# Two-layer recurrent-memory transformer: query, key and output products as 64-column pairs where the plan allows it, and seven groups of rows prepared early instead of five

## The chip, the core and the metric

The kernel runs on one core of a Trainium2 chip. The metric is the device time of one execution in microseconds (us); the time before is the median of four runs, 1634.55 us (1633.62 to 1636.03). Everything is planned when the program is built: the device executes a fixed list of instructions for each engine, without loops or branches.

## What is computed

Four blocks in a row: attention with a recurrent memory, a two-matrix feed-forward, then both again with the same weights. Cut to what matters:

```python
def A(x, mem, Wq, Wk, Wv, Wo):             # x: 2048 rows of 512, mem: 8 rows
    for s in range(64):                    # 64 segments of 32 rows, one after the other
        h = concat(mem, x[32*s:32*s+32])   # 40 rows
        q, k, v = h@Wq, h@Wk, h@Wv         # 32 heads of 128 columns
        p = softmax(masked(q @ k.T * scale))
        o = (p @ v) @ Wo                   # 40 rows of 512
        mem, out[s] = o[:8], o[8:]
def B(x): return relu(x@w1) @ w2           # 512 -> 1376 -> 512
x = x + A(norm(x)); x = x + B(norm(x))     # layer one
x = x + A(norm(x)); x = x + B(norm(x))     # layer two
```

The memory makes a chain: segment s+1 can't start before the first 8 output rows of segment s are there.

## The kernel before

**Tiling and order.** The two layers run interleaved, four segments apart (`DELTA` = 4). A step k handles segment k of layer one and segment k-4 of layer two, so there are 68 steps: 0 to 3 and 64 to 67 hold one layer, 4 to 63 hold both. In a two-layer step the two segments stand side by side as 80 columns of a tile `HT`, and one weight load serves both. The kernel keeps all four weight matrices in SBUF (4 MB each) and lives from TensorE (PE).

A step consists of: `step_values` (V = HT.T x Wv for the rows that are not prepared ahead; 64 weight columns, 512 moving columns, L973), `queries_keys` (Q and K per half unit of heads, 16 matmuls of 128 weight columns and 80 moving columns each, L1074; 16 such operations a step), `scores` (L1103, then the softmax on VectorE and ScalarE, and a transposition on PE at L646), `attend` (L1187) and `project` (32 heads x 4 column blocks into one PSUM bank, L1214). The copy at L1230 then moves the 8 memory rows of each layer to the next step's `HT`. Every second step a `finish_pair` runs the feed-forward for 64 rows of each layer (L646 and L766).

**Modes of PE.** A matmul addresses either the whole array (128 weight columns) or a part of its columns (64, or 32 in `values_narrow` at L992). Each operation is marked `WHOLE`, `COL64`, `COL32`, or `EITHER`; the last is emitted by the helper `across` (L642) as one 128-column matmul or as two 64-column ones, after the mode that PE is in. Values and scores are `COL64`; queries, keys and projections are `WHOLE`.

**The planner.** `Plan.order` (L320) simulates six resources with a cost for each operation, takes at each point the ready operation with the best priority (`PLACE`, `AHEAD`, `RULE` are numbers found beforehand), and charges `TURN` = 0.096 us for a change of PE's mode. Its result is the order in which each engine executes.

**Values prepared ahead.** Half the rows of a segment (its first 16) don't depend on the memory, so their V is computed for a group of four segments at once and stored in DRAM (`vh`), to be loaded into `V0` by a DMA in front of each step (`place_values`, L1003). Groups 0 to 5 (`EARLY` = 5) are prepared at the start, in the time in which the weights arrive, with 64-column matmuls (`early_values`, L926); the results of groups 1 to 5 wait in the room of `w1` and `w2`, which are loaded later. Groups 6 to 15 are prepared in five pairs during steps 4 to 53 (`late_values`, L937: 8 operations of 4 matmuls of 128 weight columns x 512, L944). Both kinds are `spare`: the planner may put them off. In steps 1 to 3, `values_narrow` makes the remaining V rows with 32 weight columns, evicts them into `vw`, and DMAs on SP's queue move them into `V0`.

**Start.** Weights are loaded in the order v, q/k, q/k, o, o through POOL's queue (`load_weights`, L488). Stores of the early groups follow on the same queue (L932), stores of their normalized rows `xh` on SP's queue after step 1's first loads (`put_op`), and `w1`/`w2` after that (`load_dense`, L503).

Of the kernel before, what the change touches and what calls it, by code (L numbers as in the profile page):

```python
# [26 lines left out]
WHOLE, COL64, EITHER, COL32 = range(4)  # L27
TURN = 0.096

RULE = (0.0731, 331.4491, 505.4188, 866559925356557.625)  # L30
PERIOD = 46.2777
PLACE = {
    ("attend.mmu0.0", 0): -152.667, ("attend.mmu0.0", 1): -118.912, ("attend.mmu0.0", 2): -639.225,
    ("attend.mmu0.0", 3): 328.193, ("attend.mmu0.0", 4): -173.499, ("attend.mmu0.0", 5): 386.967,
    ("attend.mmu0.0", 6): 449.133, ("attend.mmu1.0", 0): -183.38, ("attend.mmu1.0", 1): 433.744,
    ("attend.mmu1.0", 2): 361.711, ("attend.mmu1.0", 3): 441.403, ("attend.mmu1.0", 4): -122.568,
    ("attend.mmu1.0", 5): 199.077, ("attend.mmu1.0", 6): 581.404, ("attend.mmu2.0", 0): -862.741,
    ("attend.mmu2.0", 1): -762.821, ("attend.mmu2.0", 2): -99.412, ("attend.mmu2.0", 3): -218.396,
    ("attend.mmu2.0", 4): -720.778, ("attend.mmu2.0", 5): -60.014, ("attend.mmu2.0", 6): -142.579,
    ("attend.mmu3.0", 0): -166.299, ("attend.mmu3.0", 1): -129.893, ("attend.mmu3.0", 2): -1226.967,  # L40
    ("attend.mmu3.0", 3): 67.821, ("attend.mmu3.0", 4): -136.693, ("attend.mmu3.0", 5): -20.817,
    ("attend.mmu3.0", 6): 293.466, ("attend.mmu4.0", 0): 65.898, ("attend.mmu4.0", 1): -215.881,
    ("attend.mmu4.0", 2): 381.601, ("attend.mmu4.0", 3): 412.604, ("attend.mmu4.0", 4): -130.21,
    ("attend.mmu4.0", 5): -853.627, ("attend.mmu4.0", 6): 948.075, ("dense_layer.mm.0", 1): 732.94,
    ("dense_layer.mm.0", 3): 740.199, ("dense_layer.mm.0", 6): 839.326, ("dense_layer.mm.1", 1): -969.556,
    ("dense_layer.mm.1", 3): -286.677, ("dense_layer.mm.1", 6): 67.604, ("dense_layer.mm.2", 1): 398.19,
    ("dense_layer.mm.2", 3): 243.499, ("dense_layer.mm.2", 6): 419.477, ("dense_layer.mm.3", 1): 627.889,
    ("dense_layer.mm.3", 3): 181.496, ("dense_layer.mm.3", 6): 643.035, ("dense_layer.mm.4", 1): 161.37,
    ("dense_layer.mm.4", 3): 390.622, ("dense_layer.mm.4", 6): 400.054, ("dense_layer.mm.5", 1): 594.567,
    ("dense_layer.mm.5", 3): 753.248, ("dense_layer.mm.5", 6): 345.325, ("finish_pair.turn.0", 1): -144.39,  # L50
    ("finish_pair.turn.0", 3): -761.751, ("finish_pair.turn.0", 6): -878.802, ("g0", 2): -907.97,
    ("g1", 2): 259.128, ("g2", 2): -170.342, ("g3", 2): -266.685, ("g4", 2): -99.976, ("g5", 2): 565.774,
    ("late_values.mmv0.0", 0): 283.731, ("late_values.mmv1.0", 0): -248.92, ("late_values.mmv2.0", 0): -1018.714,
    ("late_values.mmv3.0", 0): 469.169, ("late_values.mmv4.0", 0): -1001.105, ("late_values.mmv5.0", 0): 1.489,
    ("late_values.mmv6.0", 0): -868.467, ("late_values.mmv7.0", 0): 433.155, ("layernorm.turn.0", 1): 337.759,
    ("layernorm.turn.0", 3): 441.922, ("layernorm.turn.0", 6): -292.588, ("layernorm.turn.1", 1): -863.663,
    ("layernorm.turn.1", 3): -167.818, ("layernorm.turnr.0", 0): -153.966, ("layernorm.turnr.0", 4): 426.349,
    ("layernorm.turnr.1", 0): 374.651, ("layernorm.turnr.1", 4): 594.017, ("prepare.turns.0", 2): -916.093,
    ("project.mm.0", 0): 352.884, ("project.mm.0", 1): 403.52, ("project.mm.0", 2): 426.265,
    ("project.mm.0", 3): 475.549, ("project.mm.0", 4): -8.363, ("project.mm.0", 5): 481.308,  # L60
    ("project.mm.0", 6): 364.213, ("project.mm.1", 0): 360.97, ("project.mm.1", 1): 250.905,
    ("project.mm.1", 2): 395.025, ("project.mm.1", 3): 90.611, ("project.mm.1", 4): -154.497,
    ("project.mm.1", 5): 342.487, ("project.mm.1", 6): -140.762, ("project.mm.2", 0): 69.475,
    ("project.mm.2", 1): 427.61, ("project.mm.2", 2): -910.526, ("project.mm.2", 3): 539.171,
    ("project.mm.2", 4): -962.774, ("project.mm.2", 5): 327.765, ("project.mm.2", 6): 570.292,
    ("project.mm.3", 0): 234.432, ("project.mm.3", 1): 212.581, ("project.mm.3", 2): 219.168,
    ("project.mm.3", 3): 1057.658, ("project.mm.3", 4): 374.948, ("project.mm.3", 5): 458.206,
    ("project.mm.3", 6): 1049.752, ("project.mm.4", 0): -906.842, ("project.mm.4", 1): -226.675,
    ("project.mm.4", 2): -119.077, ("project.mm.4", 3): 366.414, ("project.mm.4", 4): -955.316,
    ("project.mm.4", 5): 408.222, ("project.mm.4", 6): -222.974, ("queries_keys.mmu0.0", 0): -319.479,  # L70
    ("queries_keys.mmu0.0", 1): -311.142, ("queries_keys.mmu0.0", 2): -195.441,
    ("queries_keys.mmu0.0", 3): -783.942, ("queries_keys.mmu0.0", 4): -856.389,
    ("queries_keys.mmu0.0", 5): -1226.512, ("queries_keys.mmu0.0", 6): -189.749,
    ("queries_keys.mmu0.1", 0): -126.555, ("queries_keys.mmu0.1", 1): -875.245,
    ("queries_keys.mmu0.1", 2): -230.758, ("queries_keys.mmu0.1", 3): -218.806, ("queries_keys.mmu0.1", 4): -924.83,
    ("queries_keys.mmu0.1", 5): -998.214, ("queries_keys.mmu0.1", 6): -798.535, ("queries_keys.mmu0.2", 0): 1.933,
    ("queries_keys.mmu0.2", 1): -915.221, ("queries_keys.mmu0.2", 2): -763.206,
    ("queries_keys.mmu0.2", 3): -815.004, ("queries_keys.mmu0.2", 4): -155.478,
    ("queries_keys.mmu0.2", 5): -920.249, ("queries_keys.mmu0.2", 6): -766.935, ("queries_keys.mmu0.3", 0): -285.59,
    ("queries_keys.mmu0.3", 1): -134.747, ("queries_keys.mmu0.3", 2): 7.492, ("queries_keys.mmu0.3", 3): -23.601,  # L80
    ("queries_keys.mmu0.3", 4): -292.473, ("queries_keys.mmu0.3", 5): -193.042,
    ("queries_keys.mmu0.3", 6): -173.541, ("queries_keys.mmu1.0", 0): -40.306,
    ("queries_keys.mmu1.0", 1): -1010.704, ("queries_keys.mmu1.0", 2): -94.937,
    ("queries_keys.mmu1.0", 3): -233.672, ("queries_keys.mmu1.0", 4): -212.713,
    ("queries_keys.mmu1.0", 5): -961.418, ("queries_keys.mmu1.0", 6): -321.925,
    ("queries_keys.mmu1.1", 0): -965.925, ("queries_keys.mmu1.1", 1): -223.66, ("queries_keys.mmu1.1", 2): -323.504,
    ("queries_keys.mmu1.1", 3): 20.112, ("queries_keys.mmu1.1", 4): -146.653, ("queries_keys.mmu1.1", 5): -223.193,
    ("queries_keys.mmu1.1", 6): -158.937, ("queries_keys.mmu1.2", 0): -823.694,
    ("queries_keys.mmu1.2", 1): -932.252, ("queries_keys.mmu1.2", 2): -231.6, ("queries_keys.mmu1.2", 3): -250.634,
    ("queries_keys.mmu1.2", 4): 237.43, ("queries_keys.mmu1.2", 5): -250.953, ("queries_keys.mmu1.2", 6): -993.941,  # L90
    ("queries_keys.mmu1.3", 0): -189.715, ("queries_keys.mmu1.3", 1): -231.672,
    ("queries_keys.mmu1.3", 2): -257.674, ("queries_keys.mmu1.3", 3): -300.812,
    ("queries_keys.mmu1.3", 4): -145.268, ("queries_keys.mmu1.3", 5): -37.546, ("queries_keys.mmu1.3", 6): -183.014,
    ("queries_keys.mmu2.0", 0): 140.663, ("queries_keys.mmu2.0", 1): -210.356, ("queries_keys.mmu2.0", 2): -294.536,
    ("queries_keys.mmu2.0", 3): -112.732, ("queries_keys.mmu2.0", 4): 320.259, ("queries_keys.mmu2.0", 5): 215.543,
    ("queries_keys.mmu2.0", 6): -122.288, ("queries_keys.mmu2.1", 0): 428.309, ("queries_keys.mmu2.1", 1): 92.511,
    ("queries_keys.mmu2.1", 2): -899.997, ("queries_keys.mmu2.1", 3): 229.222, ("queries_keys.mmu2.1", 4): 280.866,
    ("queries_keys.mmu2.1", 5): 161.233, ("queries_keys.mmu2.1", 6): 27.508, ("queries_keys.mmu2.2", 0): 204.746,
# [82 lines left out]
    ("values_direct.ev", 1): -11.513, ("values_narrow.ev", 1): -7.969,  # L181
}

LOAD = {("v", 0): 4.4, ("v", 1): 3.8, "o": 2.95}
REST, SLOW = 2.75, 6.0

EARLY, SPREAD = 5, (0, 0, 2, 4, 4, 6, 8, 8)


def t_mm(n):  # L190
    return max(0.025, 0.0025 + n / 2400)


# [211 lines left out]
def kernel(  # L405
# [597 lines left out]
    def place_values(k, late):  # L1003

        act, seg = segs(k)
        if 0 not in act:
            return
# [344 lines left out]
```

## Time and profile before

| what | value |
|---|---|
| median of 4 runs | 1634.55 us |
| profiled execution: its time, its span | 1636.03 us, 1634.2 us |
| PE busy (matmuls) | 1590.3 us, 97% of the span |
| PEld busy (weight loads) | 1378.5 us, 84% |
| VectorE, ScalarE, GpSimd busy | 68%, 64%, 9% |
| PE clock granted | 0.997 |
| steps 0; 1 to 3; 4 to 63; 64 to 67 and the rest (ended at the copy at L1230) | 52.1; 56.5; 1441.3; 84.3 us |

The profile names PE the matmul engine and PEld its weight loads, which overlap the matmuls. Busy time of PE is not work: matmuls are pipelined, so a matmul of 80 columns shows some 200 ns from start to end while the next one starts 36 ns later. What a matmul costs in a stream is read from the distance of the starts, in the timeline. A few matmul records are missing from a trace: 39898 matmuls are recorded beside 39992 weight loads.

### The profile page before, as it was taken

The page shows a single profiled execution, that of the slowest core. Times are in us where ns is not written, and L with a number is a line of the kernel's source. Part 1 is how long each engine was busy: PE and PEld are TensorE (multiplying, and loading weights), DVE is VectorE, ACT ScalarE, POOL GpSimd, SP SyncE. Part 2 cuts the span into 40 slices and gives each one's busy share as a digit, 9 for nine tenths or more (in the row PEclk, how much of TensorE's full clock was granted, in tenths as well). Part 3 has the DMA queues.
Part 4 walks back from the last instruction along what each step waited for, and adds up shares of the span by engine and source line. Part 5 has one row for each costly group of instructions (what it writes and reads, how often), then busy time and mean ns, then how long its engine had stood idle before and what let it go on. Part 6 is the DMA issues. An engine that isn't in the chain of part 4 may idle for free.

```text
span 1634.2 us, 88442 instructions
## 1 busy us (share of the span) xinstructions
PE 1590.3 (97%) x39898; PEld 1378.5 (84%) x39992; DVE 1111.9 (68%) x3091; ACT 1052.7 (64%) x2655; POOL 139.7 (9%) x352
## 2 busy tenths in 40 slices
PE   7899999999999999999999999999999999999997
PEld 4788888888888888888888888888888888888886
DVE  4566776776676676677667667667667766766765
ACT  5566666676666666666667666666766666666664
POOL 3100000000000100000100000100000000000000
PEclk9999999999999999999999999999999999999999
DMA  9710111110110110110110111110110000000000
GB/s 371 240 39 21 23 25 27 42 27 22 28 24 22 41 26 22 25 33 18 40 29 22 28 25 28 35 28 20 28 28 24 24 21 22 18 18 18 18 6 6
DMA packets 47097, 63.89 MB, mean 39 GB/s; under 512 B 17784, under 2 KB 33440, under 8 KB 46720
## 3 DMA queue, kind: packets, MB, share of 16 engines
q1 hardware_dynamic: 41136, 39.09, 9.8%
q0 software_dynamic: 4704, 18.35, 2.9%
q8 instruction: 313, 5.13, 1.3%
q10 hardware_dynamic: 880, 0.80, 0.2%
q14 instruction: 64, 0.52, 0.1%
HBM read 33.50 MB, written 11.93 MB: 28 GB/s over the span
## 4 chain that ended last, share of the span: by engine, by line
PE 92%; DMA 4%; ACT 2%; DVE 1%; issue 1%; POOL 0%; SPq 0%; ACTq 0%; POOLq 0%; DVEq 0%
PE work L1074 36%; PE st L1214 19%; PE fill L973 13%; PE fill L646 10%; PE work L1187 4%; PE work L1103 4%; DMA Wo_sb<-in_A_Wo_dram 2%; PE work L646 2%; PE fill L944 2%; DMA xe<-in_A_x_dram 1%; ACT OT L894 1%; DVE HT L1230 0%; PE fill L766 0%; DMA vw<-in_A_x_dram 0%; PE fill L992 0%
## 5 line engine op out<-in xcount | busy, mean ns | idle before, releaser
L1074 PE MATMUL work<-HT,Wk_sb 128*128 128x80 bf16 (+1 forms) x8704 | 355.7, 199 | 9.5 <-DVE HT L1230 8.8
L1074 PE MATMUL work<-HT,Wq_sb 128*128 128x80 bf16 (+1 forms) x8704 | 349.2, 199 | 2.1 <-DVE HT L1230 0.9
L1214 PE MATMUL st<-OT,Wo_sb 128*128 128x80 bf16 (+1 forms) x8704 | 344.7, 199 | 5.2 <-ACT OT L894 2.5
L1214 PEld LDWEIGHTS <-Wo_sb 128*128 128x128 bf16 x8704 | 325.2, 99 | 28.8 <-issue 6.4
L1074 PEld LDWEIGHTS <-Wq_sb 128*128 128x128 bf16 x8704 | 320.2, 99 | 27.2 <-issue 16.0
L1074 PEld LDWEIGHTS <-Wk_sb 128*128 128x128 bf16 x8704 | 321.6, 99 | 16.3 <-DVE HT L1230 13.3
L894 ACT CAST qT<-work 128x320 bf16<-128x320 f32 (+1 forms) x534 | 219.5, 412 | 76.9 <-PE work L1074 32.6
L973 PE MATMUL fill<-Wv_sb,HT 128*64 128x512 bf16 x2048 | 265.9, 381 | 0.0
L894 ACT CAST kT<-work 128x320 bf16<-128x320 f32 (+1 forms) x510 | 209.9, 412 | 83.0 <-PE work L1074 49.6
L894 ACT CAST OT<-work 128x320 bf16<-128x320 f32 (+1 forms) x404 | 158.1, 418 | 120.3 <-PE work L1187 117.8
L1168 ACT ACTIVATE PT<-work,half 128x320 bf16<-128x320 f32 (+2 forms) x384 | 170.9, 468 | 68.2 <-PE work L646 48.8
L894 ACT CAST vw<-fill 128x512 bf16<-128x512 f32 x203 | 119.0, 586 | 91.3 <-PE fill L973 84.3
L1114 DVE TENSOR_TENSOR es<-work,maskb 128x320 f32<-128x320 f32 (+2 forms) x340 | 136.8, 404 | 44.8 <-PE work L1103 39.9
L1170 DVE TENSOR_SCALAR PT<-work,half 128x160 bf16<-128x160 f32 (+2 forms) x296 | 127.6, 454 | 26.8 <-PE work L646 24.0
L973 PEld LDWEIGHTS <-HT 128*64 128x64 bf16 x2048 | 99.0, 110 | 52.1
L1125 ACT ACTIVATE es<-es 128x320 f32<-128x320 f32 (+2 forms) x340 | 137.6, 410 | 6.1 <-DVE es L1121 5.2
L1121 DVE TENSOR_TENSOR es<-es,mx 128x320 f32<-128x320 f32 (+2 forms) x340 | 136.8, 405 | 5.4
L1118 DVE TENSOR_REDUCE mx<-es 128x8 f32<-128x320 f32 (+2 forms) x340 | 135.3, 400 | 6.2
L1145 DVE TENSOR_TENSOR P<-es,sm 128x320 bf16<-128x320 f32 (+2 forms) x340 | 133.0, 407 | 5.3
L1230 DVE CAST HT<-st 128x64 bf16<-128x64 f32 (+1 forms) x67 | 14.8, 221 | 174.9 <-PE st L1214 174.9
L1128 DVE TENSOR_REDUCE sm<-es 128x8 f32<-128x320 f32 (+2 forms) x340 | 131.6, 396 | 2.4 <-ACT es L1125 1.5
L1103 PEld LDWEIGHTS <-qT 128*40 128x40 bf16 x4096 | 91.0, 98 | 45.5 <-ACT kT L894 10.2
(98 smaller groups left out, 1781.1 us busy)
## 6 DMA issues: line engine op xcount, KB each, us to landing
V<-vw SPq DMA_DIRECT2D x252, 48.0 KB
V<-vh SPq DMA_DIRECT2D x120, 64.0 KB
vh<-vg SPq DMA_DIRECT2D x40, 128.0 KB
Wq_sb<-in_A_Wq_dram POOLq DMA_DIRECT2D x2, 2048.0 KB, 20.8
Wk_sb<-in_A_Wk_dram POOLq DMA_DIRECT2D x2, 2048.0 KB, 25.5
Wo_sb<-in_A_Wo_dram POOLq DMA_DIRECT2D x2, 2048.0 KB, 36.0
Wv_sb<-in_A_Wv_dram POOLq DMA_DIRECT2D x1, 2048.0 KB, 11.2
vh<-w_sb POOLq DMA_DIRECT2D x4, 512.0 KB, 9.4
```

What stands on the lines that cost most here:

```text
L646: nc.tensor.matmul(out_[u:v, :], lhsT=lhsT[:, u:v], rhs=rhs, start=start, stop=stop, tile_position=(0, u))
L894: nc.scalar.copy(out=out_, in_=in_)
L973: nc.tensor.matmul(vp[64 * b:64 * b + 64, :], lhsT=cols(c4), rhs=Wv_sb[:, c4, n * 512:(n + 1) * 512], start=(c4 == 0), stop=(c4 == NC4 - 1 ...
L1074: nc.tensor.matmul(qp[:, hi * 2 * L:hi * 2 * L + n], lhsT=W_sb[:, c4, h * Dh:(h + 1) * Dh], rhs=HT[:, c4, c0:c1], start=(c4 == 0), stop=(c ...
L1103: nc.tensor.matmul(v[64 * g2:64 * g2 + L, a, i, b, :], lhsT=qT[:, hi, a * L:(a + 1) * L], rhs=kT[:, hi, a * L:(a + 1) * L], start=True, st ...
L1114: nc.vector.tensor_tensor(out=flat(es[:, A]), in0=flat(sp[:, A]), op=ALU.add, in1=maskb[:, a_lo:a_hi, :].unsqueeze(2).to_broadcast([128, n ...
L1118: nc.vector.tensor_reduce(out=mx[:, As], in_=es3(), axis=AX.X, op=ALU.max)
L1121: nc.vector.tensor_tensor(out=es3(), in0=es3(), op=ALU.subtract, in1=mx[:, As].unsqueeze(2).to_broadcast([128, ns * na, L]))
L1125: nc.scalar.activation(out=es[:, A], in_=es[:, A], func=ACTF.Exp, scale=SCALE)
L1145: (nc.gpsimd if eng == POOL else nc.vector).tensor_tensor(out=o, in0=flat(es[:, A]), op=ALU.mult, in1=sm[:, As].rearrange("p (a s) -> p a ...
L1168: nc.scalar.activation(out=o, in_=i, func=ACTF.Copy, scale=half[:, b:b + 1])
L1214: nc.tensor.matmul(wo[:, 2 * W * c4 + c0:2 * W * c4 + c1], lhsT=Wo_sb[:, h, c4 * 128:(c4 + 1) * 128], rhs=OT[:, h, c0:c1], start=(h == 0 a ...
```

## The change

- **Pairs.** A fourth mark `SOFT` takes the place of `COL32`. In two-layer steps, queries/keys and projections are `SOFT`: if the operation's name and the step's parity are in a new table `PAIRED`, it is handled as `EITHER`, otherwise as `WHOLE`. Even steps have 8 of their 16 query/key operations in the table, odd steps 11 of 16 and three of the five projection operations (80 of 128 matmuls). `late_values` becomes `EITHER`.
- **A planned rate of fetch.** Each PE operation tells the planner its number of matmuls (`count`, doubled when an `EITHER` operation runs as pairs). The planner lets no four blocks of 64 matmuls pass in under 7.0 us.
- **Early groups.** `EARLY` goes from 5 to 7; group 6 waits in `vg`, group 7 in `vw`. The early values of group 0 go. Four pairs of groups are left to prepare late, 12 steps apart from step 6 on. All stores of early groups (rows and values) go to POOL's queue, those of three groups after step 0's first attention, the others after step 1's first scores; `load_dense` no longer waits for `loaded`.
- **Steps 0 to 3** compute 64 columns of V straight into `V0` for every step; `values_narrow`, `values_direct` and the DMAs of those steps go.
- `RULE`, `PERIOD`, `PLACE` and `AHEAD` have new numbers.

```diff
-WHOLE, COL64, EITHER, COL32 = range(4)
+WHOLE, COL64, EITHER, SOFT = range(4)
 TURN = 0.096
+BLOCK, FETCH = 64, 7.0
...
+PAIRED = {
+    ("project.mm.1", 1), ("project.mm.2", 1), ("project.mm.4", 1), ("queries_keys.mmu0.0", 0),
...
-EARLY, SPREAD = 5, (0, 0, 2, 4, 4, 6, 8, 8)
+EARLY, SPREAD = 7, (0, 0, 2, 4, 4, 6, 8, 10)
...
+        o.soft = tile == SOFT
+        o.tile = o.mode = tile if not o.soft else EITHER if (o.key, phase(o.step)) in PAIRED else WHOLE
...
-                o.mode = o.tile if o.tile != EITHER else WHOLE if tile == COL32 else tile
+                o.mode = o.tile if o.tile != EITHER else tile
+                n, t1 = o.count * (1 + (o.mode == COL64 and o.tile == EITHER)), t
+                for i in range(issued // BLOCK + 1, (issued + n) // BLOCK + 1):
+                    t1 += max(0.0, blocks[-4] + FETCH - (t1 + o.cost[e] * (i * BLOCK - issued) / n))
+                    blocks = [*blocks[-3:], t1 + o.cost[e] * (i * BLOCK - issued) / n]
+                issued, o.end = issued + n, t1 + o.cost[e]
...
-                     r=["loaded", ("sc", k, u), *[("room", g, p) for g, p in room_users(i // 4)]], w=[("w", i)])
+                     r=[("sc", k, u), *[("room", g, p) for g, p in room_users(i // 4)]], w=[("w", i)])
...
+    def early_stores(gate):
+
+        g, put_x, xnT = stores.pop(0)
+        bulk(POOL, 0.78, put_x, ("xh", g), 0.125, r=gate, w=[("xh", g)], uses=on(xnT))
+        for p0, n in ((0, 2), (2, 2)) if g == 5 else ((0, 4),):
             def put(p0=p0, n=n):
                 nc.gpsimd.dma_start(out=vh[g][:, p0:p0 + n, :], in_=room_span(g, p0, n))
...
-        if k == 0:
-            values_direct(HTs[0][:, :, 0:L], deps)
-            return
-        if 1 in act:
-            values(lambda c4: HTs[i][:, c4, HS:2 * L], lambda p: vw[:, p, :], ("vw",), deps)
+        if k < DELTA:
+            values(lambda c4: HTs[i][:, c4, 0:64], lambda p: V0[:, p, :], lambda p: [("V0", p, b) for b in range(2)], deps)
         else:
-            values_narrow(HTs[i][:, :, HS:HS + 32], deps)
-        place_values(k, False)
+            values(lambda c4: HTs[i][:, c4, HS:2 * L], lambda p: vw[:, p, :], lambda p: [("vw", p)], deps)
+            place_values(k, False)
...
-            def mm(qp=qp, W_sb=W_sb):
+            def mm(cols=128, qp=qp, W_sb=W_sb):
                 for hi, h in enumerate(heads):
                     for c4 in range(NC4):
-                        nc.tensor.matmul(qp[:, hi * 2 * L:hi * 2 * L + n], lhsT=W_sb[:, c4, h * Dh:(h + 1) * Dh],
-                                         rhs=HT[:, c4, c0:c1], start=(c4 == 0), stop=(c4 == NC4 - 1))
+                        across(cols, qp[:, hi * 2 * L:hi * 2 * L + n], W_sb[:, c4, h * Dh:(h + 1) * Dh],
+                               HT[:, c4, c0:c1], start=(c4 == 0), stop=(c4 == NC4 - 1))
...
-    start = {g: DELTA + 10 * i for i, g in enumerate(pairs)}
+    start = {g: DELTA + 2 + 12 * i for i, g in enumerate(pairs)}
...
+                while stores:
+                    early_stores([("sc", 1, 0)])
                 load_dense(k, u)
...
+        while k == 0 and len(stores) > EARLY - 3:
+            early_stores([("att", 0)])
```

## The prediction

> **What bounds the kernel now.** I read the page first: its first lines, and part 4, the chain that ended last.
>
> ```profile
> span 1634.2 us, 88442 instructions
> PE 1590.3 (97%) x39898; PEld 1378.5 (84%) x39992; DVE 1111.9 (68%) x3091; ACT 1052.7 (64%) x2655; POOL 139.7 (9%) x352
> ...
> PE 92%; DMA 4%; ACT 2%; DVE 1%; issue 1%; POOL 0%; SPq 0%; ACTq 0%; POOLq 0%; DVEq 0%
> ```
>
> PE alone carries the chain; VectorE and ScalarE have a third of the time free. So only what PE does between the first and the last matmul counts: stream work, changes of mode, waits. Then the table by stage, cut at the copies of L1230 that end steps 0, 3 and 63 (start:end, length, busy time of each engine):
>
> ```profile
> 0.00:52.10 52.10, 41.37 (x713) 26.76 (x713) 25.51 (x83) 28.10 (x61) 18.45 (x43) 1.00 0.99 371
> 52.10:108.60 56.50, 50.73 (x1578) 43.66 (x1579) 33.05 (x131) 32.98 (x113) 6.76 (x16) 0.97 0.42 122
> 108.60:1549.90 1441.30, 1422.88 (x35411) 1243.70 (x35503) 1005.82 (x2691) 945.60 (x2330) 110.64 (x283) 1.00 0.11 26
> ```
>
> The 30 pairs of two-layer steps take 1441.3 us, 48.04 each. Last the timeline of PE, for starts (start, length, matmuls):
>
> ```profile
> 721.47 1.31 PE L1074 MATMUL work<-HT,Wq_sb 128*128 128x80 bf16 x32
> 722.61 0.31 PE L646 MATMUL work<-ident,P 128*128 128x80 bf16 x4
> 722.85 0.38 PE L1103 MATMUL work<-kT,qT 128*40 128x40 bf16 x16
> ```
>
> 32 matmuls from 721.47 to 722.61 are 36 ns each. Four more should end at 722.75, but the column-tiled scores start at 722.85: the change of mode costs some 0.1 us; the planner's 0.096 fits, and I take it. Counted in the timeline, steps 4 to 63 have 304 changes, 29.2 us. They border 152 whole-array stretches. 60 hold a projection and stay, one a step. The other 92 hold queries and keys with operations that are `EITHER` now or become so; only queries and keys force the mode there. A pair of steps also waits some 0.49 us for the memory, from the last projection to the copy at L1230, in the step that has no feed-forward to cover it.
>
> **Part 1, pairs: what a pair costs.** Before has this shape already, in `attend`: 64 weight columns, 80 moving ones.
>
> ```profile
> 700.51 0.23 PE L1187 MATMUL work<-PT,V 128*64 128x80 bf16 x2
> 700.55 0.23 PE L1187 MATMUL work<-PT,vw 128*64 128x80 bf16 x2
> 700.58 0.23 PE L1187 MATMUL work<-PT,V 128*64 128x80 bf16 x2
> 700.62 0.23 PE L1187 MATMUL work<-PT,vw 128*64 128x80 bf16 x2
> ```
>
> Each x2 is a pair, and pairs start every 36 ns: a pair is as long as the whole matmul that it replaces. Longer runs agree: 32 feed-forward matmuls of 64 x 128 take 27.6 ns each, 55 a pair, against 56 for one whole matmul. So a paired operation costs 0 in stream time, whether in a query or a projection. The weight loads of a pair:
>
> ```profile
> L1187 PEld LDWEIGHTS <-vw 128*128 128x128 bf16 x652 | 50.2, 100 | 0.2
> L1187 PEld LDWEIGHTS <-vw 128*64 128x64 bf16 x744 | 31.3, 112 | 3.8 <-ACT vw L894 0.2
> ```
>
> Half the columns take longer to load, yet the starts stay 36 ns apart, so the loads hide. (A rule speaks against the change here: the Trainium skill, "TensorEngine Tiling (Array Packing)", section "Restrictions and Gotchas", has column tiling exclude the fast weight load. With the price that "TensorE: Matmul & The Clock Gate" gives in "LDWEIGHTS (loading the stationary operand)", columns over 1.2 in ns, two loads of 64 columns in a row would be an estimated 107 ns a pair; that would make this change hundreds of us slower. The 36 ns in the rows above decide against it.)
>
> **What pairs save.** A stretch goes only if all queries and keys in it are in the table. Of 32 such operations in two steps, 19 are; 13 stay whole (8 in even, 5 in odd steps) and need a stretch of their own or room next to the projections. Bounds: none of the 92 goes (0), or all (92 x 2 x 0.096 = 17.7 us). I take 19/32, 55 stretches: **-10.6 us**.
>
> **Part 2, instruction fetch.** 5.13 MB in 313 packets of the instruction queue are 16.4 KB each, and over the 79890 recorded PE instructions 64 bytes an instruction: a packet holds 128 matmuls with their loads. Between packet starts I find 3.33 us at the least, 26 ns a matmul. That fetch can stall PE shows in step 2:
>
> ```profile
> 82.90 0.19 PE L1214 MATMUL st<-OT,Wo_sb 128*128 128x40 bf16 x1
> 85.13 0.65 PE L1214 MATMUL st<-OT,Wo_sb 128*128 128x40 bf16 x19 [2.04 <-issue]
> ```
>
> No wait of the program ends here; a packet starts at 82.83, ends at 83.86, and PE goes on 1.3 us later. The same pattern stands at 52.9 (0.96 us). Both fall among one-layer matmuls every 25 ns. (The Trainium skill, "Runtime: NRT & Kernel Launch", section "Instruction fetch mechanics", has the same 16 KiB blocks, but calls the crossing mostly hidden; by that this part would cost nothing, and the two stalls show otherwise.) Pairs start every 18 ns, faster than 26. If every operation of the table ran as pairs, it would add (19 x 16 + 80) x 30 = 11520 matmuls: 35503 + 11520 = 47023 in 1441 us, 30.7 ns each. The average fits, and the values (108 ns a matmul) lie among the pairs; bursts may not fit. Bounds: 0, or every one of 11520 pairs at the fetch rate, 52 ns against 36: 11520 x 16 ns = 184 us. Nearest are steps 4 to 63 of before, where I find no such stall; with the margin down from 40.6 to 30.7 ns I take **+2 us**.
>
> **Part 3, a pair of groups less to prepare late.** 8 operations of 4 matmuls at 0.216 us are 6.9 us, 8 transposes at 0.056 make it 7.4. But the spare matmuls also fill waits: the copy at L1230 returns every 48.2 us between 276.9 and 518.0, and every 47.5 between 1338.0 and 1527.8, where none are left. 0.77 x 5 pairs of steps are 3.9 us. Bounds -7.4 and -3.9; I take **-5 us**.
>
> **Part 4, start.** PE does more: two groups of values more and group 0 less (+3.5 us: 4 x 4 pairs x 0.216), and in steps 1 to 3 values with 64 instead of 32 columns (+1.73 each, +5.2): +8.7. Against it: from 8.6 to 108.6 us PE waits some 14 us, and spare values can fill part; `Wo` lands at 50.23 now, after stores that 43.05 to 48.70 put among the weights; some 1.2 MB at 346 GB/s (the rate of that stretch) are 3.5 us that it gains. Bounds: +8.7 if nothing fills, -3.5 if all fill; I take **+4 us**.
>
> **Parts costed at nothing.** Steps 1 to 3 lose 18 DMAs on SP's queue (0.8 us each to issue); no wait of the chain of steps 1 to 3 is for them. The stores move to POOL: 15 issues of 0.56 us, and a store that waits for the attention or the scores holds back what is queued behind it there, the copies into `HT` and the norm's power steps; POOL is 9% busy and those run a step ahead. `w1`/`w2` must wait for stores: 4.6 MB at 346 GB/s, the last 2.6 MB from 59.1 on (step 1's first scores), end near 67; 2.8 MB of `w1` and `w2` follow until about 75, and the feed-forward first uses them at 80.3. If these 5 us go, each us of delay reaches step 4, because layer two's first segment comes from there. The last four steps have no pairs: 0. The 0.49 us wait for the memory, 14.6 us over 30 pairs of steps, remains by my account: new priorities may move either way, and I put 0 for it, with -7 as the far case.
>
> **Sum**, against the profiled execution (1636.03 us, 1.8 of them outside the span): -10.6 + 2 - 5 + 4 = -9.6, so 1626.4. The median shown is 1.5 lower, so **1625 us**.
>
> **Rivals.** *Larger gain*: all 92 stretches go (-17.7), the late groups bring their full 7.4, waits at the start swallow the new work, half of the memory waits fill (-7): -32, about 1602. For it: 19 of 32 operations could leave just enough buffers to gather the other 13 beside the projections. Against it: two-layer steps have a ring of four query and four key buffers, and 8 whole operations in an even step can hardly all sit in one place.
> *Fetch takes the place of the mode changes*: pairs cluster with scores (13 ns a matmul) and PE runs dry. Price 16 ns a pair. Without part 2 the sum is -11.6 us; at 725 starved pairs, 6% of 11520, it is gone, and at 930 the kernel is slower by 3.3. A fifth starved is 37 us: about 1660; a tenth 18: 1641. For it: 82.90. Against it: the average of 30.7 ns, and fewer pairs where PE happens to be whole.
> *It does little*: `EITHER` only follows the mode. If most paired operations still run whole, 304 changes stay, and parts 3 and 4 give -1: 1634.
> *Late start*: `w1`/`w2` slip past 80.3 and nothing fills: 1640.
>
> **How the numbers follow.** About 0.2% (3.3 us) is what a measurement can tell from no change. Forecast, 1613 to 1631: 0.54. Larger gain: 0.17. Little: 0.09. Fetch: 0.13, late start 0.07, both slower. So faster 0.71, same 0.09, slower 0.20. The range leaves out half of the larger gain and the worse half of the slower cases: **1604 to 1643**.
>
> **What would show it.** Right: fewer changes of mode in steps 4 to 63 (about 194), rows of L1074 and L1214 with 128*64 loads and pairs 36 ns apart, the copies at L1230 closer than 48.0 us a pair of steps, 32 late operations at L944 instead of 40, step 3 ending near 112. Wrong: waits of 1 to 2 us marked issue, in front of matmuls that wait for nothing and close to packets of the instruction queue (fetch); pairs more than 36 ns apart (loads); step 4 late behind the feed-forward.

## The result: 1631.8 us, a little over a third of the forecast gain

The changed kernel takes 1631.8 us (median; 1630.41 to 1633.64), the kernel before, run beside it, 1635.37 us (1631.41 to 1639.24). The ratio is 0.9979, with a 95% interval from 0.9974 to 0.9984: faster by 0.21%, where 0.6% was forecast. The profiled execution has a span of 1629.7 us, 4.5 less than before's 1634.2.

The first lines of the page of the changed kernel, and its chain of work that ended last:

```profile
span 1629.7 us, 94544 instructions
PE 1586.6 (97%) x43116; PEld 1379.8 (85%) x43179; DVE 1046.2 (64%) x3025; ACT 1079.3 (66%) x2717; POOL 139.8 (9%) x363
...
PE 93%; DVE 4%; issue 1%; ACT 1%; DMA 1%; POOL 0%; DVEq 0%; POOLq 0%; ACTq 0%; SPq 0%
```

PE still carries the chain, now with 3187 more weight loads (43179 for 39992). The same table by stage as in the prediction, cut at the copies into `HT` (L1212 now) that end steps 0, 3 and 63 (start:end, length, then busy time of PE, PEld, DVE, ACT and POOL):

```profile
0.00:56.54 56.54, 43.93 (x741) 28.36 (x743) 25.93 (x80) 29.88 (x68) 21.09 (x49) 1.00 0.97 359
56.54:112.58 56.04, 52.86 (x1559) 43.70 (x1559) 34.76 (x134) 32.61 (x110) 9.95 (x23) 1.00 0.32 108
112.58:1543.03 1430.45, 1414.14 (x38673) 1243.75 (x38733) 935.38 (x2619) 971.55 (x2393) 104.91 (x281) 1.00 0.11 25
1543.03:1629.71 86.68, 75.69 (x2148) 63.99 (x2149) 50.16 (x192) 45.22 (x146) 3.86 (x10) 0.95 0.02 6
```

Steps 4 to 63 are 10.9 us shorter (1441.3 before), steps 0 to 3 are 4.0 longer (108.6 before), and the last four steps with what follows 2.4 longer (84.3 before). Split by what PE does, with each load counted at the length of its matmul (two column-tiled loads side by side count as one), each change of mode at 0.096 us, and the remainder as waits:

| steps 4 to 63 | length | work | changes of mode | waits |
|---|---|---|---|---|
| before | 1441.3 | 1380.5 | 304 (29.2 us) | 31.6 |
| after | 1430.45 | 1374.8 | 244 (23.4 us) | 32.25 |

Sixty changes of mode are gone, 30 stretches, and not 55. What runs as pairs is seen in the weight loads of these steps (loads, busy time, mean ns):

```profile
L667 PEld LDWEIGHTS <-Wo_sb 128*128 128x128 bf16 x7680 | 291.1, 100 | 7.8 <-issue 1.5
L667 PEld LDWEIGHTS <-Wq_sb 128*128 128x128 bf16 x6656 | 256.3, 100 | 11.9 <-DVE HT L1212 5.1 <-issue 1.6
L667 PEld LDWEIGHTS <-Wk_sb 128*128 128x128 bf16 x6240 | 238.7, 100 | 12.3 <-DVE HT L1212 11.7 <-DVE HT L1217 0.2
L667 PEld LDWEIGHTS <-Wk_sb 128*64 128x64 bf16 x2880 | 63.3, 112 | 12.3
L667 PEld LDWEIGHTS <-Wq_sb 128*64 128x64 bf16 x2048 | 41.7, 113 | 0.0
```

4928 loads of 64 columns are 2464 pairs, in 154 of the 960 query and key operations; no projection is ever a pair. Of the 19 query and key operations in the table some five run as pairs in two steps. The others, and all projections in it, are `EITHER` and stand in stretches that are whole anyway.

### The profile page after: what moved, and what is told of

It reads as the page before. It is cut to its first block, busy times and chain, and to the rows that moved or that the text cites. A ratio compares the mean times of both kernels' runs of the same rounds, so it can differ in the third digit from the quotient of the medians.

```text
span 1629.7 us, 94544 instructions
## 1 busy us (share of the span) xinstructions
PE 1586.6 (97%) x43116; PEld 1379.8 (85%) x43179; DVE 1046.2 (64%) x3025; ACT 1079.3 (66%) x2717; POOL 139.8 (9%) x363
## 4 chain that ended last, share of the span: by engine, by line
PE 93%; DVE 4%; issue 1%; ACT 1%; DMA 1%; POOL 0%; DVEq 0%; POOLq 0%; ACTq 0%; SPq 0%
PE work L667 38%; PE st L667 19%; PE fill L1000 16%; PE fill L667 12%; PE work L1168 4%; PE work L1084 3%; DVE es L1095 1%; DVE sm L1109 1%; DVE mx L1099 1%; DVE P L1126 0%; DVE HT L1212 0%; DVE es L1102 0%; PE fill L791 0%; DMA xb<-in_A_x_dram 0%; ACT OT L921 0%
## 5 line engine op out<-in xcount | busy, mean ns | idle before, releaser
L667 PE MATMUL work<-HT,Wk_sb 128*128 128x80 bf16 (+2 forms) x10144 | 363.4, 200 | 9.7 <-DVE HT L1212 9.2
L667 PE MATMUL work<-HT,Wq_sb 128*128 128x80 bf16 (+2 forms) x9728 | 361.5, 200 | 0.4 <-issue 0.2
L667 PEld LDWEIGHTS <-Wk_sb 128*128 128x128 bf16 (+1 forms) x10144 | 330.7, 103 | 29.6 <-DVE HT L1212 12.8
L667 PEld LDWEIGHTS <-Wq_sb 128*128 128x128 bf16 (+1 forms) x9728 | 326.9, 102 | 13.5 <-DVE HT L1212 5.1
L921 ACT CAST kT<-work 128x320 bf16<-128x320 f32 (+1 forms) x537 | 219.8, 410 | 71.2 <-PE work L667 35.1
L921 ACT CAST qT<-work 128x320 bf16<-128x320 f32 (+1 forms) x484 | 197.8, 409 | 102.5 <-PE work L667 58.5
L1149 ACT ACTIVATE PT<-work,half 128x160 bf16<-128x160 f32 (+2 forms) x447 | 203.0, 469 | 17.9 <-DVE PT L1151 14.0
L921 ACT CAST vw<-fill 128x512 bf16<-128x512 f32 x229 | 134.2, 586 | 104.2 <-PE fill L1000 102.1
L1151 DVE TENSOR_SCALAR PT<-work,half 128x320 bf16<-128x320 f32 (+2 forms) x233 | 105.1, 455 | 44.0 <-PE work L667 42.1
L1212 DVE CAST HT<-st 128x64 bf16<-128x64 f32 (+1 forms) x67 | 14.8, 221 | 163.4 <-PE st L667 163.1
L1168 PE MATMUL work<-PT,vw 128*64 128x80 bf16 (+1 forms) x1384 | 105.9, 202 | 1.7 <-DVE PT L1151 1.7
```

The source lines that it names most:

```text
L667: nc.tensor.matmul(out_[u:v, :], lhsT=lhsT[:, u:v], rhs=rhs, start=start, stop=stop, tile_position=(0, u), **more)
L921: nc.scalar.copy(out=out_, in_=in_)
L1149: nc.scalar.activation(out=o, in_=i, func=ACTF.Copy, scale=half[:, b:b + 1])
L1151: nc.vector.tensor_scalar_mul(out=o, in0=i, scalar1=half[:, b:b + 1])
L1168: nc.tensor.matmul(o[u:u + cols, :, a, :], lhsT=V[:, p, e0 + u:e0 + u + cols], rhs=PT[:, a, 2 * i + h2, :, :], start=True, stop=True, tile ...
```

## The experiments

Theory 1: the steady gain is changes of mode at 0.096 us each, fewer of them than forecast, plus the late pair. Theory 2, a rival: a floor of some 47.4 us per two steps, set by the chain of waits through the softmax and the memory (latency) and not by PE's work, takes up what PE saves. Theory 3: instruction fetch holds pairs back. The start and the end of the kernel were tried by themselves.

### The changed kernel without its pairs

```
-                o.fn(64 if o.mode == COL64 else 128)
+                o.fn(64 if o.mode == COL64 and not o.soft else 128)
```

> The changed kernel with its order of work kept, but every query and key operation issued as whole matmuls, so that 127 more changes of mode stand in steps 4 to 63 (367 instead of 240) and 2464 matmuls fewer. Theory 1 (a change of mode costs 0.096 us wherever it stands, and PE is the bound): steps 4 to 63 take 127 x 0.096 = 12.2 us more, 1442.7 instead of 1430.45, so about 1644 in all. Theory 2 (a floor of latency of some 47.4 us per pair of steps takes up part of what PE saves): clearly less, 3 to 7 us more, because the waits of 0.43 and 0.32 us shrink. Theory 3 (instruction fetch holds the pairs back): less than theory 1 too, but with stalls in the changed kernel that vanish here.

Measured: ratio to before 1.0053 (1.0039 to 1.0067), 1643.2 us. Steps 4 to 63 take 1442.75 us, 12.3 more, with 128 more changes of mode in the trace: 0.096 us each on average. Waits are 31.8 us, against 32.25. So the pairs of the change cost nothing in the stream and nothing in fetch, and they pay per change removed. Without them the new order would be 1.4 us slower here than the old one: it has 372 changes of mode against 304. More than half of what the pairs save (68 of the 128 changes) only makes good what the new order adds.

### More pairs in the same order

All remaining stretches of steps 4 to 63 that hold no projection are turned into pairs (`more_pairs`), or only those of the odd steps (`odd_pairs`, the same with the condition that the step is odd), or everything that can be paired (`all_pairs`).

```
+    def pair_up(ops, keep=()):
+        run = []
+        for o in [o for o in ops if o.eng == PE] + [None]:
+            if o is not None and o.mode == WHOLE:
+                run.append(o)
+                continue
+            if all((p.soft or p.tile == EITHER) and p.kind not in keep for p in run):
+                for p in run:
+                    p.mode = COL64
+            run = []
+        return ops
...
-        for o in plan.order():
+        for o in pair_up(plan.order(), ("project.mm",)):
```

> The changed kernel, same order, with all queries and keys in stretches that hold no projection issued as pairs: 120 changes of mode left in steps 4 to 63 instead of 240, 44040 matmuls there instead of 38692 (5216 more pairs). Theory 1: 120 x 0.096 = 11.5 us less, steps 4 to 63 in 1418.9, 1620 in all. Theory 2: the waits grow by as much as the changes shrink; at least 1422 (30 x 47.4), more likely 1426 to 1430, so 1627 to 1632 in all. Theory 3: with some 18 ns between the starts of paired matmuls against 26 ns a matmul of fetch, up to 5216 x 16 ns = 83 us more, and issue waits of 1 to 2 us in the steady steps.

> The changed kernel, same order, with pairs added only in the stretches of odd steps that hold queries and keys but no projection: 180 changes of mode instead of 240 and 41212 matmuls instead of 38692 in steps 4 to 63. Changes of mode alone: 60 x 0.096 = 5.8 us less, steps 4 to 63 in 1424.7, 1626 in all. Instruction fetch at the 14 ns per added pair that the version with pairs everywhere showed (73 us over 5216 pairs): 2400 x 14 = 34 us more, less 5.8, 1660 in all. If a supply of fetched instructions left by the even steps covers part of it, between the two.

> The changed kernel, same order, with every query, key, projection and other operation that can be paired issued as pairs in steps 4 to 63: 70 changes of mode instead of 240, and 61580 matmuls instead of 38692, one per 23.2 ns at the old time. Theory 3 (packets of 128 matmuls come no closer than 3.3 us, 26 ns a matmul): 61580 x 26 = 1601 us for steps 4 to 63, 1800 in all, with packets 3.3 us apart from end to end. Theory 1 alone: 170 x 0.096 = 16.3 us less, 1615 in all. Theory 2: 1627 to 1632.

Measured:

| kernel | ratio to before | steps 4 to 63 | loads there | changes | waits |
|---|---|---|---|---|---|
| after | 0.9979 | 1430.45 | 38731 | 244 | 32.25 |
| odd_pairs | 1.0085 (1.0068 to 1.0102) | 1448.0 | 41252 | 184 | 55.5 |
| more_pairs | 1.0361 (1.0344 to 1.0379) | 1492.2 | 44084 | 124 | 105.5 |
| all_pairs | 1.2106 (1.2074 to 1.2139) | 1774.1 | 61562 | 64 | 398.3 |

Fewer changes of mode, and slower each time. The waits grow by 23, 73 and 366 us; over the added pairs these are 9, 14 and 16 ns a pair. Theory 3 holds for pairs added to an order that was not planned for them. (No run takes the planned rate of fetch out of the change, so whether that rule is what keeps the changed kernel free of such waits is not shown.) Where PE waits is seen in `all_pairs`, PE's timeline in a row of pairs that wait for no other engine:

```profile
802.43 0.74 PE L667 MATMUL work<-HT,Wk_sb 128*64 128x80 bf16 x32
803.00 1.21 PE L667 MATMUL work<-HT,Wq_sb 128*64 128x80 bf16 x58
805.38 0.30 PE L667 MATMUL work<-HT,Wq_sb 128*64 128x80 bf16 x6 [1.16 <-issue]
805.50 0.74 PE L667 MATMUL work<-HT,Wk_sb 128*64 128x80 bf16 x32
```

An operation of 64 matmuls breaks off after 58 and goes on 1.16 us later; the releaser is only "issue". The waits view of this kernel has it as the first entry of PE's weight loads (us in total, times, longest):

```profile
PEld L667 <- issue: 313.5, 360, 1.8
```

In `odd_pairs` the same happens in the middle of an operation of eight transposes:

```profile
1550.55 0.28 PE L667 MATMUL work<-ident,P 128*64 128x80 bf16 x5
1551.34 0.26 PE L667 MATMUL work<-ident,P 128*64 128x80 bf16 x3 [0.52 <-issue]
```

The places are no accident. I numbered PE's instructions in the order of the program (a load and a matmul each, and a few others) and matched them with the recorded loads, which are complete. In `all_pairs`, 371 of the 429 gaps over 0.3 us in steps 4 to 63 stand before instruction 193 to 195 of a block of 256; in `more_pairs` 96 of 147, in `odd_pairs` 39 of 97, in the next kernel 83 of 162. In the changed kernel itself there are 2 of 72. The gaps at these places add up to 371, 78, 25 and 73 us: all that the waits grew by. 256 instructions of 64 bytes are one packet of the instruction queue. PE goes on 2.4 us (median) after a packet starts, and where it had to wait, the next packet starts 1.15 us later: with both, 3.6 us per block of 128 matmuls. `all_pairs` has its packets 3.68 us apart (median), 28.8 ns a matmul, and 1774 us over 61562 loads are 28.8 ns too. In the changed kernel the blocks of steps 4 to 63 last 2.8 us or more, but for one of some 2.7 with a wait before the next. Single blocks of 2.3 us passed without a wait in `more_pairs`, after slower ones; so some 3 us a block is a rule for blocks in a row, read from these runs.

(The Trainium skill, "Runtime: NRT & Kernel Launch", section "Instruction fetch mechanics", has the block of 256 instructions fetched while the one before it executes. The places of the gaps agree. It calls the crossing mostly hidden; here that holds for the changed kernel, and not for rows of blocks that PE could run through in 2.3 us each, as it would with pairs 18 ns apart.)

### Only the pairs, in the old order

The kernel before, with queries and keys through `across(cols, ...)`, and `pair_up` over its own order (`before_pairs`: all stretches that can be converted; `short_pairs`: late values too are made convertible, and only stretches with fewer than three query and key operations are taken).

```
+        o.soft = o.kind.split(".")[0] in ("queries_keys", "late_values") and PE in o.cost and DELTA <= o.step < STEPS
...
+            if sum(p.kind[:13] == "queries_keys." for p in run) < 3 and all(p.soft or p.tile == EITHER for p in run):
```

> The kernel before with its own order, and only the pairs of the change: the 66 stretches of steps 4 to 63 that hold no projection and no late values have their queries and keys issued as pairs (6912 matmuls more); 170 changes of mode instead of 302. Theory 1: 132 x 0.096 = 12.7 us less, steps 4 to 63 in 1428.6 instead of 1441.3, 1622 in all. Theory 2: half of it or less, 1435 or more. Theory 3: stalls, up to 6912 x 16 ns = 111 us more.

> The kernel before with its own order, and pairs only in the 30 stretches of the odd steps that hold two query and key operations and no projection (two such operations, an attention and at times a transposition or a late value each): 242 changes of mode instead of 302 in steps 4 to 63, as many fewer as the change has, with some 1300 matmuls more. If 0.096 us a change is all, and a stretch this short (2.3 us with its attention, fewer than 128 matmuls) brings no wait for instructions: 60 x 0.096 = 5.8 us less, steps 4 to 63 in 1435.5 instead of 1441.3, 1629.5 to 1630 in all. If every added pair costs the 10 to 14 ns that the long stretches showed: 13 to 18 us more, less 5.8, so 1643 to 1648. If waits for latency take up what PE saves: 1438 or more, above 1632 in all.

Measured, `before_pairs`: ratio 1.0374 (1.0353 to 1.0394); steps 4 to 63 in 1500.6 us with 172 changes of mode; the waits go from 31.6 to 103.6 us, again at the block ends. Converted here are 30 stretches of six and 30 of eight query and key operations (96 and 128 pairs; the 96 follow one another without a break), and six of two operations.

`short_pairs`: ratio 0.9966 (0.9954 to 0.9978), 1628.07 us. Steps 4 to 63 take 1435.66 us, 5.65 less than before, with 244 changes of mode; waits are 31.7 (31.6 before). That is theory 1 to 0.2 us, with no wait for instructions: two operations between values at 108 ns a matmul do not use up a block. In the net it is also what the change does, although there 154 operations run as pairs, in a new order, and here 60 in the old one. The two operations of an odd step in the kernel before:

```profile
1303.05 1.03 PE L973 MATMUL fill<-Wv_sb,HT 128*64 128x512 bf16 x8
1304.30 0.75 PE L1074 MATMUL work<-HT,Wq_sb 128*128 128x80 bf16 x16
1304.88 0.74 PE L1074 MATMUL work<-HT,Wk_sb 128*128 128x80 bf16 x16
```

in `short_pairs`:

```profile
1295.71 1.03 PE L974 MATMUL fill<-Wv_sb,HT 128*64 128x512 bf16 x8
1296.86 0.74 PE L647 MATMUL work<-HT,Wq_sb 128*64 128x80 bf16 x32
1297.43 0.74 PE L647 MATMUL work<-HT,Wk_sb 128*64 128x80 bf16 x32
```

and in the changed kernel:

```profile
1296.24 1.03 PE L1000 MATMUL fill<-Wv_sb,HT 128*64 128x512 bf16 x8
1297.10 0.74 PE L667 MATMUL work<-HT,Wk_sb 128*64 128x80 bf16 x32
1297.67 0.74 PE L667 MATMUL work<-HT,Wq_sb 128*64 128x80 bf16 x32
```

16 whole matmuls of 0.74 us have become 32 of 64 columns in the same 0.74 us, and the two changes of mode around them are gone. An even step has four changes before and after; an odd step has six before and four after. `short_pairs` is the fastest of the kernels that compute everything: its span is 1625.9 us, 3.8 shorter than the change's, although the intervals of the two ratios still overlap. It keeps the old start and end; what else the change brings shortens steps 4 to 63 by another 5.2 us and costs more than that at the start and the end.

### What a late operation costs

> The changed kernel that leaves out three of the four matmuls of each of the 32 late operations (the late values are then sums over a quarter of the columns), 96 matmuls of 0.2165 us, 20.8 us of PE work. If late work is on the path in full: steps 4 to 63 in 1409.7 instead of 1430.45. If it fills waits as the spacing of the copies suggested (3.9 of 7.4 us per pair of groups are paid): 11 us less, 1419.5. The prediction's value (5 of 7.4) would give 14 us less, 1416.4.

```
-            for c4 in range(NC4):
+            for c4 in range(1):
...
-                       Wv_sb[:, c4, n * 512:(n + 1) * 512], start=(c4 == 0), stop=(c4 == NC4 - 1))
+                       Wv_sb[:, c4, n * 512:(n + 1) * 512], start=True, stop=True)
```

Measured: ratio 0.9956 (0.9941 to 0.9970), 1627.35 us; steps 4 to 63 in 1428.0 us. Of 20.8 us of work taken away, 2.5 came back. All three expected numbers were far off. In the changed kernel the late operation stands before transposes of `P` and hides their wait (first fence); with a quarter of it left, PE waits 0.40 us for `P` (second fence):

```profile
248.09 1.03 PE L667 MATMUL fill<-Wv_sb,xnE 128*64 128x512 bf16 x8
248.96 0.31 PE L667 MATMUL work<-ident,P 128*64 128x80 bf16 x8
```

```profile
247.50 0.39 PE L667 MATMUL fill<-Wv_sb,xnE 128*64 128x512 bf16 x2
248.29 0.34 PE L667 MATMUL work<-ident,P 128*64 128x80 bf16 x8 [0.40 <-DVE P L1126]
```

So there is a floor of the kind that theory 2 supposes, in the odd steps, which have no feed-forward. Their mean length by the number of late operations that they hold, from the copies into `HT` (number of steps in brackets):

| odd steps | none | one | two |
|---|---|---|---|
| before | 22.09 (6) | 22.47 (10) | 23.01 (14) |
| short_pairs | 22.09 (6) | 22.25 (10) | 22.80 (14) |
| after | 22.09 (6) | 22.17 (16) | 22.70 (8) |

Without a late operation an odd step lasts 22.09 us whether it has six changes of mode or four: there latency sets the end, and the two changes are worth nothing. With one or two, PE sets it, and the two changes are worth 0.21 to 0.22 us. The 0.096 us above is thus a mean over steps that gain about 0.105 us a change and steps that gain nothing. The first late operation of a step costs 0.08 to 0.4 us, the second some 0.54, though each is 0.87 us of work.

### The start

> The changed kernel with five early groups instead of seven and the old start steps of the late groups (a pair of late groups every 10 steps from step 4), all else as in the change. If the early groups act as the prediction says: step 0 to 3 shorter by at most the 6.9 us of PE work of two groups (2 x 4 x 0.866) and at least by 2 where waits take its place; steps 4 to 63 longer by the work of one late pair, 7.4 us, less what falls into waits (3.9 at the least), plus some 10 more changes of mode, 1.0 us: 1435 to 1439. In all 1631 to 1637. If the start of the change is late for another reason (the first x load, which lands at 6.8 us instead of 4.8), the start shortens by less than 3 us and the whole is slower than the change by 2 to 5 us.

```
-EARLY, SPREAD = 7, (0, 0, 2, 4, 4, 6, 8, 10)
+EARLY, SPREAD = 5, (0, 0, 2, 4, 4, 6, 8, 8)
...
-    start = {g: DELTA + 2 + 12 * i for i, g in enumerate(pairs)}
+    start = {g: DELTA + 10 * i for i, g in enumerate(pairs)}
```

Measured: ratio 1.0128 (1.0109 to 1.0147), 1656.2 us. Steps 0 to 3 do 5.4 us less work and take 114.0 us, 1.4 more; steps 4 to 63 take 1456.8, with waits of 52 us. It does not tell the theories apart, because the planner makes a new order with numbers that were found for another. It only shows that two groups fewer do not by themselves shorten the start.

> The changed kernel with one priority changed: the load of x for group 0 is issued first on ScalarE's queue again, ahead of the load for group 1. If the order of these two loads is why the start is 4 us longer, the norm of group 0 starts at 4.8 us instead of 6.8, the first values before 10.5 instead of 12.6, and the end of step 3 comes 2 to 4 us earlier; the whole at 1628 to 1630. If the work of the two more groups is the cause, step 3 ends as before, at 112 to 113, and the whole stays at 1631 to 1632.

```
+AHEAD["prepare.get_x", 1] = 1000.0
```

Measured: ratio 1.0034 (1.0023 to 1.0045), 1641.3 us. The first values run at 11.39 us, but step 3 ends at 119.9: one priority re-planned the whole start, with 1.1 and 0.6 us of waits in step 0's softmax and waits of 1.3, 1.9 and 2.5 us, all three before instruction 195 of a block. So the next kernel keeps the order and exchanges two entries of it:

```
+    def x_first(ops):
+        i, j = sorted(n for n, o in enumerate(ops) if (o.kind, o.group) in (("prepare.get_x", ""), ("*prepare_group.load", "1")))
+        ops[i], ops[j] = ops[j], ops[i]
+        return ops
```

> The changed kernel with its order kept and only two neighbours on ScalarE's queue exchanged: the load of x for group 0 goes out before that for group 1. If the 2 us by which the norm of group 0 starts late (6.8 instead of 4.8 us) are carried to the end of the start: first values at 10.6 to 11.6 instead of 12.6 us, step 0 and step 3 end 1 to 2 us earlier, 1630 to 1631 in all. If the weights set the start (Wo lands at 51.25 us) or instruction fetch does, step 3 still ends at 112 to 113 and the whole stays at 1631.5 to 1632.

Measured: ratio 0.9964 (0.9950 to 0.9978), 1630.7 us. What the exchange does at the beginning, first the changed kernel, then `x_swap` (start, length, the norm of group 0's x and the first values of a group):

```profile
6.80 0.69 DVE L708 BATCH_NORM_STATS2 ln<-xb 128x6 f32<-128x512 bf16 x1 [1.62 <-DMA xb<-in_A_x_dram]
...
12.62 2.77 PE L1000 MATMUL fill<-Wv_sb,xg 128*64 128x512 bf16 x12 [0.68 <-ACT xg L921]
```

```profile
5.09 0.68 DVE L708 BATCH_NORM_STATS2 ln<-xb 128x6 f32<-128x512 bf16 x1
...
10.63 2.77 PE L1000 MATMUL fill<-Wv_sb,xg 128*64 128x512 bf16 x12 [0.68 <-ACT xg L921]
```

The 2 us come in as expected, step 0 ends 2.6 us earlier (53.97), step 3 1.7 earlier (110.92); steps 1 to 3 give back 0.9 in waits. How much of it lasts is not settled. The changed start, run in six kernels that differ only after it, ends step 3 at 111.25 to 113.23 us (mean 112.2), and the kernel before ends it at 106.88 to 109.08 in three (mean 108.2). The difference of 4.1 us is clear of this spread; a gain of 1.7 in one profile is not.

### The end

> The changed kernel, in which the last four steps (64 to 67) take the priorities of the kernel before. If the new numbers are the cause of the 2.4 us that the end lost, the end goes from 86.7 to 84.3 us and the whole from 1631.8 to 1629.4, with the waits of 1.07 us before the transposed attention of steps 65 and 66 gone. If the end is late for what comes before it, it stays at 86 to 87.

```
+PLACE.update(END_PLACE)
+AHEAD.update(END_AHEAD)
...
-                o.prio = PERIOD * o.step + PLACE.get((o.key, phase(o.step)), 0.0)
+                o.prio = PERIOD * min(o.step, STEPS) + END_PERIOD * max(o.step - STEPS, 0) + PLACE.get((o.key, phase(o.step)), 0.0)
```

(`END_PLACE` and `END_AHEAD` are the entries of the kernel before for these steps.)

Measured: ratio 0.9976 (0.9966 to 0.9985), 1631.55 us; the end takes 85.67 us, 1.0 less. In the changed kernel, the wait of step 65:

```profile
1576.80 0.27 PE L667 MATMUL work<-ident,P 128*128 128x80 bf16 x3
...
1577.93 0.38 PE L1168 MATMUL work<-PT,vw 128*128 128x80 bf16 x6 [0.87 <-DVE PT L1151]
```

It is gone with the old numbers, and step 65 is 16.49 us again (16.41 before, 17.60 after). But there is a new wait in `after_old_end` at the end of step 66, before the first queries of step 67:

```profile
1601.66 0.39 PE L712 MATMUL work<-HT,Wq_sb 128*128 128x40 bf16 x9 [0.68 <-DVE HT L1257]
```

> Both edits on the changed kernel: the load of x for group 0 first, and the priorities of the kernel before in the last four steps. If they add up: 1 to 2 us at the start and 1.0 us at the end (as the run with the old end showed in its last stage), 1629 to 1630.5 in all. If the start gains nothing, 1631.

Measured: ratio 0.9973 (0.9964 to 0.9982), 1631.1 us. They do not add up: the end gains 0.7 us (86.0), step 3 ends at 113.3. With the old numbers the end takes 85.7 and 86.0 us, under the eight profiles with the changed end (86.2 to 87.1, mean 86.8): some 0.9 of the 2.4 us goes with the new numbers, in its last stretch. Up to the copy that ends step 66 the last steps take 55.7 us in the changed kernel, 53.6 in the kernel before and 56.1 in `after_old_end`, so nothing is gained there. The rest stays open.

## Why the prediction was wrong in size, step by step

**Sum.** In profiled spans -10.6 + 2 - 5 + 4 = -9.6 was forecast, and -4.5 came: -5.65 for the pairs, nothing for fetch, -5.2 for the late pair and the new order together, +4.0 for the start, +2.4 for the end (and 0.05 of rounding).

**Pairs cost nothing, a change of mode 0.096 us.** Right: `whole_same_order` puts 128 changes at 12.3 us, `short_pairs` 60 at 5.65, though not evenly: nothing in the six odd steps without a late operation.

**"I take 19/32, 55 stretches."** This is the step that failed most: 30 stretches went in the net, -5.65 us in place of -10.6. The 92 stretches of the kernel before are 30 of eight query and key operations in the even steps, 30 of six and 30 of two in the odd ones, and 2 in step 4; in the changed kernel an odd step has one stretch without a projection, of five operations, in place of two. A table entry lets an operation follow the mode; it does not make it a pair, and most entries follow the whole mode. The share of operations in the table says nothing of the share of stretches: a stretch goes when all its operations go, and in these runs only short ones went at a gain: with longer ones as pairs too (`before_pairs`, `odd_pairs`, `more_pairs`), the waits for instructions grew by more than the changes saved. Both were to be had before the run: the rival "It does little" said that `EITHER` only follows the mode, and the stretches could have been sorted by length.

**Fetch, +2.** It measured 0 in the changed kernel. The price in the rival, 16 ns a pair, is what unplanned pairs cost (9 to 16). The two stalls read in the profile of before, at 52.9 and 82.90 us, stand before instruction 194 of a block. My measure, the mean time of a matmul over the whole kernel, was the wrong one: `more_pairs` has 32 ns on average without its waits at block ends, well above the 28.8 that fetch sustains in `all_pairs` (26 was my reading), and loses 73 us. The bound holds over a few blocks of 128 matmuls, and not over the mean of the kernel.

**A late pair less, -5.** Near in size, -5.2 (what steps 4 to 63 gained beyond the 5.65), but by luck. I counted eight operations; two of the 40 ran ahead of step 4 in the kernel before (L944 at 103.1 and 103.8 us), so these steps lose six, and six odd steps go from two to one. At the 0.55 us between the rows of `short_pairs` that is 3.3 us. The other 1.9 us are there because steps with as many late operations are 0.08 to 0.10 us shorter than in `short_pairs`; no run parts the new order from the late pair. It is also not that part of each operation falls into waits: the first of a step does almost wholly, the second by about a third.

**Start, +4.** Right in size, 4.0, by luck; the reasons were not right. The claim that `Wo` lands 3.5 us earlier once the stores leave its queue is refuted: the stores were queued behind it, and it lands at 51.25 us, 1.0 later. The work grew by 7.1 us in place of 8.7, since the two late operations (1.7 us) left this stretch; 12 changes of mode went (1.15 us), and waits fell by 2.0, although the first load of x, which I had not looked at, adds 2 us of them at the very beginning. How far the rest is work and how far waits for instructions stays open.

**Last four steps, 0.** Wrong: +2.4. "They have no pairs" was true and beside the point, since all priorities were new. Some 0.9 us goes with the new numbers; in that are four changes of mode more (29 in place of 25), by count some 0.4 us. The rest stays open.

**Parts at nothing in the steady steps.** The wait for the memory is 0.49 us as before, and waits as a whole moved by 0.7 us. The loads of `w1` and `w2`, forecast to land near 75 us, landed at 83 to 91, and the feed-forward began at 89.6 in place of 80.3: the first half of the rival "Late start" came true. No wait of PE for them stands in steps 2 to 4; whether the late feed-forward costs anything is not shown.

## What to carry to other kernels

Count what has to vanish together: a saving per stretch goes by stretches that vanish whole, not by the operations in them, and the shortest stretches are the ones to take first. More and smaller matmuls were free here only while blocks of 256 PE instructions that follow one another lasted about 3 us each; look at the fetch bound block by block, since a mean over the kernel hides it. Work put into a step that waits for latency is free up to the length of its wait, so spread it, one piece a step, before counting its whole length as cost.

## What the runs showed of the hardware that I had not expected

PE waits for its instructions at fixed places, every 256 instructions of the program, in the middle of operations that wait for nothing else; in `all_pairs` at 371 of the 481 blocks of steps 4 to 63. The time from the start of a packet to the next instruction is 2.4 us (median), of which moving the 16 KB takes 1.0. In steps 1 to 3, where the weights still come in, the waits at these places add up to some 2 to 3 us in six runs of the changed start and 2 to 4 in three of the old one; the end of step 3 differs by as much between executions of one and the same order (111.25 to 113.23 us and 106.88 to 109.08).
